# An adaLN transformer block on one core: packed head rows, 11-matmul output projections, and where two of four blocks are projected

## The chip, the cores and the metric

The kernel runs on one core of a Trainium2 chip. The metric is the device time of one execution in microseconds. The engines are named as in the profile: PE (TensorE, matmuls), PEld (the weight loads of TensorE), DVE (VectorE), ACT (ScalarE), POOL (GpSimd) and SP (SyncE, which here only issues DMAs).

## The reference, cut to what matters

One sequence of 2048 tokens with 448 features passes through attention with 16 heads of 28 and then through an MLP of width 1792. Both are modulated by six rows computed from a condition `c`:

```python
sa, ca, ga, sb, cb, gb = (silu(c) @ w_mod).reshape(1, 6, 1, 448) rows
h = layernorm(x) * (1 + ca) + sa
x = x + ga * (softmax_attention(h, wqkv, heads=16) @ wo)     # heads side by side: 448 columns
h = layernorm(x) * (1 + cb) + sb
x = x + gb * (gelu(layernorm(h) @ w1 + b1) @ w2 + b2)
```

The change touches the product of the attention's output with `wo` and the addition to `x`.

## The kernel before, in words

**Precision.** Large products run in the fp32r format. An operand is split into `hi` (the value rounded to fp32r) and `lo` (the rest), and a product is summed as hi·hi + hi·lo + lo·hi. So each piece of 128 contracted rows costs three matmuls.

**Phase 1** (the first 166 us of the profile) computes the modulation, the layernorm, the queries, keys and values, and a first part of the row maxima of the scores. Queries and keys go through DRAM, in tiles that hold four heads, each head in 32 rows of which 28 are data.

**Attention** is a loop of 16 units of 16 steps (`for u in range(NU)`, L1271). Unit `u` is head group `g = u // 4` (four heads) and query block `qt = u % 4` (512 tokens); its 16 steps `kt` go over tiles of 128 keys. Below, a step's number is `16 * u + kt`, 0 to 255. A step issues 12 score matmuls (L1305) into two PSUM pairs, two exponentials on ACT (L1318), between them some matmuls whose only use is a later row maximum (L476, reduced on DVE at L481), and then the four products with the values (L1263, `av`) of the step before. Everything else hangs on steps through `at(step, fn)` and a dictionary `sched`: after the `av` of a step, the functions planned for it are emitted. All instructions of an engine run in the order of emission; waits come from data and buffers.

From step 121 on (`RING`) a third PSUM pair is in use for the scores, except in the steps for which `is_wo` holds (L1239): there the third pair is given back, so that its two banks can take other matmuls. When no maxima are left (`three`), the third pair is used throughout. Which maxima go into which step is set by `extra` and `emit_single`, three of them in a step of this phase.

**End of a unit** (`unit_end_tasks`, L995). The unit's output, 4 heads by 32 rows by 512 queries, of which row 28 of each head holds the softmax's denominators, is normalised in four tasks: `t_den` and `t_rec` send the denominators through DRAM and broadcast their reciprocals, `t_split` multiplies (POOL, L1019), `t_split2` makes `hi` (DVE if the unit's output is stored, ACT if not, L1029) and `lo` (POOL, L1030). For groups 0 to 2 the pair is stored to DRAM (`doh`, L1034: two DMAs of 128 rows, gap rows included), except unit (2, 3), whose output stays on chip. Stored units run their tasks 1, 4, 10 and 11 steps into the next unit, the others 1, 2, 6 and 7.

**Output projection before** (`t_wo`, L1036). When the last group of a query block is normalised, the three stored groups of that block have been loaded again (`load_o`, six DMAs of 256 KB, L992), and four chains, one for each 128 tokens, multiply them with `wo_p`, which is `wo` with `ga` folded in, in the same layout of four heads in 128 rows with gaps. A chain has 4 groups of 3 terms, 12 matmuls of 128 rows by 448 columns; ACT copies it out of PSUM (L1052) and POOL adds it to the residual `acc` (L1053). Blocks 0, 1 and 2 are projected at `kt` 8 to 11 of units 13, 14 and 15, one chain in a step. Block 3 has two parts: the groups 0 to 2 (9 matmuls a chain) at `kt` 8 to 11 of unit 12, and group 3 (3 matmuls a chain) after the attention.

**MLP** (L1398). `seq` goes over 4 blocks of 14 slices, and iteration `n` emits `mlp1` of slice `n` (11 matmuls of 512 columns, L396 and L1347, then GELU), the functions that `tail` holds for `n`, one or two items of weight preparation (`w_prep`: load, split into hi and lo), the next block's layernorm stages, and `mlp2` of slice `n - 2` (12 matmuls of 448 columns, L1389 to L1391). The first `mlp1` is emitted before the last `av`. `tail` holds the eight tasks of the last unit: before, at `n` = 0, 0, 4, 5 for the normalising and 9, 10, 11, 12 for the four chains of 3. The PSUM banks for `mlp1`, for chains and for transposes are a ring of three.

**Weight preparation** starts in unit 15 (`w_prep`, L1220): ten of its items are done in steps 245 to 255, each with a load two items ahead into a ring of three `raw` buffers, then two or three operations on DVE (L1150, L1151, L1169 to L1172). Items go into the slots that attention leaves (`a0` to `e1`), so a slot that is taken for something else must be free again by its item. SP issues every one of these DMAs in order, and stops at the first that has to wait.

Of the kernel before, what the change touches and what calls it, by code (L numbers as in the profile page):

```python
# [44 lines left out]
def tile_adaln_block(ctx: ExitStack, tc: tile.TileContext, x, wqkv, wo, w1, b1, w2, b2, c, w_mod, out):  # L45
# [72 lines left out]
    def f(t):  # L118
        return t.bitcast(F32)
# [834 lines left out]
                self.n += 1  # L954
            self.load(self.n + 2)

    def wo_item(g):
        def ld(r):
            pool.memset(r[:, :D], 0.0)
            for j in range(4):  # L960
                hd = 4 * g + j
                sp.dma_start(r[32 * j : 32 * j + DH, :D], wo[DH * hd : DH * hd + DH, :])

        def go(r):
            full = sbt("full", [128, 512], bufs=3)
            pool.tensor_tensor(out=full[:, :D], in0=r[:, :D], in1=rows["ga"], op=ALU.mult)

            def rest():
                dve.tensor_copy(wo_p[0][:, g, :], full[:, :D])
                pool.tensor_tensor(out=wo_p[1][:, g, :], in0=full[:, :D], in1=f(wo_p[0])[:, g, :], op=ALU.subtract)  # L970

            at(6 + 2 * g, rest)

        return ld, go

    doh = [
        [dr.tile([128, S], F32R, tag=f"o{part}{g}", name=f"o{part}{g}", bufs=1) for g in range(NG - 1)]  # L980
        for part in range(2)
    ]
    o_in = {}

    def last_g(qt):
        return NG - 2 if qt == NB - 1 else NG - 1

    def load_o(qt):
        for g, tag in zip(range(last_g(qt)), ("a2h", "a3h", "b1h")):
            t = slot(tag, [128, 2, 512])  # L990
            for part in range(2):
                sp.dma_start(f(t)[:, part, :], f(doh[part][g])[:, qt * 512 : (qt + 1) * 512])  # L992
            o_in[(qt, g)] = t

    def unit_end_tasks(u, o_sb):  # L995
        g, qt = divmod(u, NB)
        st = {}
        staged = g < last_g(qt)
        parts = [g] if g > last_g(qt) else list(range(g + 1))

        def t_den():
            q_ = pool if u == NU - 1 else sp
# [18 lines left out]
        def t_split2():  # L1021
            on = st["on"]
            if u < NU - 1:
                hi = sbt("hi", [128, 512], F32R, bufs=3)
                lo = sbt("lo", [128, 512], F32R, bufs=3)
            else:
                hi = sb.tile([128, 512], F32R, tag=YTAGS[7], name="o_hi", bufs=1)
                lo = sbt("osb", [128, 512], F32R, bufs=2)
            (dve.tensor_copy if staged else act.copy)(hi, on)  # L1029
            pool.tensor_tensor(out=lo, in0=on, in1=f(hi), op=ALU.subtract)  # L1030
            st["hi"], st["lo"] = hi, lo
            if staged:
                for part in range(2):
                    sp.dma_start(f(doh[part][g])[:, qt * 512 : (qt + 1) * 512], f((hi, lo)[part]))  # L1034

        def t_wo(t):  # L1036
            def go():
                if t == 3 and mx_ring[0] == "m1" and len(mx_ring) > 1:
                    mx_ring.append(mx_ring.pop(0))
                p = ps_mx()  # L1040
                ts = slice(t * 128, (t + 1) * 128)
                terms = []
                for g_ in parts:
                    if g_ == g:
                        hi, lo = st["hi"][:, ts], st["lo"][:, ts]
                    else:
                        hi, lo = o_in[(qt, g_)][:, 0, ts], o_in[(qt, g_)][:, 1, ts]
                    w_hi, w_lo = wo_p[0][:, g_, :], wo_p[1][:, g_, :]
                    terms += [(hi, w_hi), (hi, w_lo), (lo, w_hi)]
                mm_acc(p[:, :D], terms)  # L1050
                y = sbt("full", [128, 512], bufs=3)[:, :D]
                act.copy(y[:, :D], p[:, :D])  # L1052
                pool.tensor_tensor(out=acc[qt][:, t, :], in0=acc[qt][:, t, :], in1=y[:, :D], op=ALU.add)  # L1053

            return go

# [123 lines left out]
    def at(step, fn):  # L1180
        sched.setdefault(step, []).append(fn)

    wo_prep = Prep([wo_item(g) for g in range(NG)])
    at(0, lambda: wo_prep.load(2))
    for g in range(NG):
        at(4 + 2 * g, wo_prep.step)

    def b2_load():
        rows["b2"] = raw_t()
# [13 lines left out]
    at(12, b2_load)  # L1203
    at(28, b2_mul)
    last0 = NKT * (NU - 1)
    lnst = [ln2_stages(b) for b in range(NB)]
# [134 lines left out]
    def mlp1(b, i):  # L1341
# [114 lines left out]
```

## Time and profile before

| what | us |
|---|---|
| median of 3 runs (1108.62 to 1109.58) | 1109.07 |
| the profiled execution, its own time | 1109.11 |
| its span, from the first to the last instruction | 1107.1 |
| steps 0 to 255 of attention | 166.7 to 812.9 |
| MLP after it | 812.9 to 1107.1 |

The granted clock of TensorE was 1.0 throughout. A busy share of PE is not PE at its peak, since matmuls are pipelined: what a stage costs is read from the time between the same instruction of one step and of the next. Times in rows are microseconds from the span's start; a group's row has its count, the busy time, the mean duration in ns, and the idle time before it with what ended it.

### The profile page before, as it was taken

Reading aid. Unit: us, or ns where it says so; the run is one execution under the profiler, and the core shown is the slowest. Engines: PE = TensorE matmul, PEld = TensorE weight load, DVE = VectorE, ACT = ScalarE, POOL = GpSimd, SP = SyncE. Lnnn points to the kernel's source line nnn. Section 1 sums busy time; section 2 is a strip of 40 time slices with the busy share of each in tenths; the row PEclk is TensorE's granted clock in tenths of the full one; section 3 lists DMA queues with packets and bytes.
Section 4 is the critical chain, followed back from the end, with each engine's and each line's share of the span. In section 5 each row is a group of like instructions: output and inputs, shape, how many; then the busy total and the mean of one; then the engine's idle time right before and its main releaser. Section 6 shows DMA issues by size and latency. Waiting matters only on the chain.

```text
span 1107.1 us, 20699 instructions
## 1 busy us (share of the span) xinstructions
PE 1097.3 (99%) x8319; PEld 666.5 (60%) x8319; DVE 799.5 (72%) x1375; ACT 703.8 (64%) x897; POOL 212.4 (19%) x214
## 2 busy tenths in 40 slices
PE   8999999999999999999999999999999999999998
PEld 6756675444444444444444454545568888888887
DVE  6968788999899989988888868584557744534322
ACT  4565667888888888888888878687764411111210
POOL 1543333110000000000000011216215414023000
PEclk9999999999999999999999999999999999999999
DMA  9563263121221201231211412022222100000000
GB/s 309 206 188 107 90 199 112 56 68 30 79 87 50 78 30 49 69 96 49 75 44 47 137 30 87 1 87 72 78 82 67 31 34 1 7 28 1 34 1 34
DMA packets 49341, 81.19 MB, mean 73 GB/s; under 512 B 12311, under 2 KB 18702, under 8 KB 49234
## 3 DMA queue, kind: packets, MB, share of 16 engines
q1 hardware_dynamic: 48762, 79.14, 22.9%
q8 instruction: 65, 1.06, 0.4%
q10 hardware_dynamic: 148, 0.46, 0.1%
q0 software_dynamic: 336, 0.28, 0.1%
q14 instruction: 30, 0.25, 0.1%
HBM read 55.04 MB, written 26.48 MB: 74 GB/s over the span
## 4 chain that ended last, share of the span: by engine, by line
PE 97%; DVE 1%; DMA 1%; ACT 1%; issue 0%; SPq 0%; ACTq 0%; DVEq 0%
PE o L1263 23%; PE s L1305 23%; PE m L396 17%; PE pa L396 9%; PE m L476 8%; PE s L1390 3%; PE s L1391 3%; PE s L1389 3%; PE s L476 2%; PE t L1390 1%; PE t L1391 1%; PE t L1389 1%; DMA slot_c<-in_w_mod_dram 1%; PE o L277 1%; DVE mxp L481 1%; PE ma L476 0%
## 5 line engine op out<-in xcount | busy, mean ns | idle before, releaser
L481 DVE TENSOR_REDUCE mxp<-m 128x1 f32<-128x512 f32 x563 | 364.6, 685 | 75.0 <-PE m L476 56.2
L1305 PE MATMUL s<-slot_b,slot_a 28*128 28x512 f32 (+1 forms) x3072 | 356.7, 423 | 0.3 <-ACT slot_c0h L1318 0.3
L1305 PEld LDWEIGHTS s<-slot_b,slot_a 28*128 28x128 f32 (+1 forms) x3072 | 210.7, 184 | 171.9 <-ACT slot_c L1318 93.9
L476 PE MATMUL m<-kh,qh 28*128 28x512 f32 x615 | 228.2, 468 | 0.5 <-DVE mxp L481 0.3
L1318 ACT ACTIVATE slot_c<-s 128x1024 f32<-128x1024 f32 x170 | 174.7, 1028 | 52.4 <-PE s L1305 51.7
L1263 PE MATMUL o<-slot_c,v 128*32 128x512 f32 x680 | 178.9, 605 | 0.0
L1351 ACT ACTIVATE full<-m,b_col 128x512 f32<-128x512 f32 x56 | 38.5, 688 | 193.7 <-PE m L396 172.5
L1263 PE MATMUL o<-slot_c1h,v 128*32 128x512 f32 x512 | 134.7, 605 | 0.0
L1263 PE MATMUL o<-slot_c0h,v 128*32 128x512 f32 x512 | 134.7, 605 | 0.0
L1318 ACT ACTIVATE slot_c0h<-s 128x1024 f32<-128x1024 f32 x128 | 131.7, 1029 | 2.5 <-PE m L396 2.5
L1318 ACT ACTIVATE slot_c1h<-s 128x1024 f32<-128x1024 f32 x128 | 130.8, 1022 | 0.0
L686 DVE TENSOR_REDUCE mxp<-s 128x2 f32<-128x1024 f32 x103 | 126.2, 1225 | 4.9 <-PE s L1305 0.3
L1354 DVE CAST hi<-full 128x512 fp32r<-128x512 f32 x42 | 18.6, 443 | 121.2 <-ACT full L1351 121.2
L1318 ACT ACTIVATE slot_d<-s 128x1024 f32<-128x1024 f32 x86 | 88.4, 1028 | 25.6 <-PE s L1305 25.5
L476 PEld LDWEIGHTS m<-kh,qh 28*128 28x128 f32 x615 | 91.5, 182 | 15.8 <-DVE mxp L481 13.4
L1263 PE MATMUL o<-slot_d,v 128*32 128x512 f32 x344 | 90.5, 605 | 0.4 <-ACT osb L1227 0.4
L1019 POOL TENSOR_TENSOR osb<-osb,osb 128x512 f32<-128x512 f32 x16 | 20.5, 1283 | 363.3 <-DMA osb<-drec 197.2
L396 PE MATMUL m<-y,slot_a 128*128 128x512 f32 x160 | 60.7, 395 | 0.0
L1355 DVE TENSOR_TENSOR lo<-full,hi 128x512 fp32r<-128x512 f32 x56 | 41.7, 745 | 20.5 <-ACT hi L1354 16.6
L481 DVE TENSOR_REDUCE mxp<-ma 128x1 f32<-128x512 f32 x61 | 39.5, 681 | 13.2 <-PE m L476 8.1
L650 DVE CUSTOM_DVE_ANT_0 slot_d0i<-m,slot_d0i 128x512 f32<-128x512 f32 x54 | 37.3, 691 | 15.2 <-PE m L476 11.4
L1263 PEld LDWEIGHTS o<-slot_c,v 128*32 128x32 f32 x680 | 24.5, 108 | 39.3 <-issue 36.8
(344 smaller groups left out, 1855.3 us busy)
## 6 DMA issues: line engine op xcount, KB each, us to landing
slot_b<-d SPq DMA_DIRECT2D x32, 256.0 KB
slot_a<-d SPq DMA_DIRECT2D x32, 256.0 KB
d<-lo SPq DMA_DIRECT2D x28, 256.0 KB
d<-hi SPq DMA_DIRECT2D x16, 256.0 KB
osb<-drec SPq DMA_DIRECT2D x15, 256.0 KB
out_dram<-xn SPq DMA_DIRECT2D x16, 224.0 KB
raw<-in_B_w_dram SPq DMA_DIRECT2D x14, 224.0 KB
qh<-d SPq DMA_DIRECT2D x12, 256.0 KB
```

The costliest lines, as they stand in the source:

```text
L396: pe.matmul(p, a, b, start=(i == 0), stop=(i == len(terms) - 1))
L476: pe.matmul(m, qh_sb[(g, qt)][js, i * 128 : (i + 1) * 128], k[js, :], start=True, stop=True)
L481: dve.tensor_reduce(out=mxp[(g, qt)][:, i, j, cch : cch + 1], in_=m, op=ALU.max, axis=AX.X)
L686: dve.tensor_reduce(out=mxp[(g, qt)][:, i, j : j + 2, cch], in_=t, op=ALU.max, axis=AX.X)
L1263: pe.matmul(o[32 * j : 32 * j + 32, :], v_sb[kt // 4][:, kt % 4, 4 * g + j, :], p[j // 2][:, j % 2, :], start=(kt == 0), stop=(kt == NKT - 1),
L1305: pe.matmul(s2[:, jj, :], ks[rows_, kp, kc], qs[rows_, qp, :], start=(term == 0), stop=(term == 2))
L1318: act.activation(pt[hf], s2, AF.Exp, scale=SCALE)
L1351: act.activation(gf, p, AF.Gelu_apprx_tanh, bias=b1_col[:, i : i + 1])
L1355: dve.tensor_tensor(out=glo, in0=gf, in1=f(ghi), op=ALU.subtract)
L1389: pe.matmul(pp, ghi[:, ts], w_hi, start=(m == 0), stop=False)
L1390: pe.matmul(pp, ghi[:, ts], w_lo, start=False, stop=False)
L1391: pe.matmul(pp, glo[:, ts], w_hi, start=False, stop=(m == NFT - 1))
```

## The change

Stored heads are packed: `dpk` in DRAM has 28 rows for each of the 12 stored heads, 336 in all, for `hi` and for `lo`. The 336 rows are two full tiles of 128 and a rest of 80. The rest's three terms are mixed into two operands: one has 80 rows of `hi` and 48 of `lo`, the other 32 rows of `lo` and 80 of `hi`, each with the fitting rows of `wo`. So a chain has 6 + 2 matmuls for the stored heads and 3 for the last group, which keeps its gaps: 11. `wo` is prepared in five items with the same layout.

Storing a unit takes four DMAs of 28 rows for each of `hi` and `lo` in place of one of 128. A block is loaded with one DMA for the full tiles of `hi`, one for those of `lo`, and four for the mixed operands.

Blocks 0 and 1 stay in units 13 and 14. Unit (2, 3) is now stored like the others, and no chain runs in unit 12. Unit (3, 2), the one with number 14, is stored too (`down`), no chain runs in unit 15, and block 2 is projected with four chains of 11 at `n` = 1 to 4 of the MLP; its mixed operands and `down` are loaded, just ahead of the first `mlp1`, into slots that the exponentials used (`c1`, `c0h`). Block 3 is projected with four chains of 11 at `n` = 6, 7, 8 and 8. For blocks 2 and 3 DVE adds the chain in PSUM to `acc` itself. `is_wo` holds in units 13 and 14 alone. `b2_load` moves from step 12 to 15.

```diff
+    NP = (NG - 1) * 4 * DH
+    MIX_HI = ((256, NP), (256, 304))
+    MIX_LO = ((304, NP), (256, NP))
...
+    dpk = [dr.tile([NP, S], F32R, tag=f"o{part}", name=f"o{part}", bufs=1) for part in range(2)]
+    down = [dr.tile([128, 512], F32R, tag=f"w{part}", name=f"w{part}", bufs=1) for part in range(2)]
...
+    def load_o(qt, n, tag):
+        t = slot(tag, [128, 2, 512])
+        o_in[(qt, n)] = t
+        cs = slice(qt * 512, (qt + 1) * 512)
+        if n < 2:
+            sp.dma_start(f(t), f(dpk[n])[0:256, cs].rearrange("(k p) n -> p k n", p=128))
+        elif n == 2:
+            for k, pieces in enumerate((zip((0, 1), MIX_HI), zip((1, 0), MIX_LO))):
+                p0 = 0
+                for part, (r0, r1) in pieces:
+                    sp.dma_start(f(t)[p0 : p0 + r1 - r0, k, :], f(dpk[part])[r0:r1, cs])
+                    p0 += r1 - r0
+        else:
             for part in range(2):
+                sp.dma_start(f(t)[:, part, :], f(down[part]))
+
+    def wo_terms(qt, own):
+        hi, lo, mix = (o_in[(qt, n)] for n in range(3))
+        w_hi, w_lo = wo_p
+        terms = []
+        for k in range(2):
+            terms += [(hi[:, k], w_hi[:, k, :]), (hi[:, k], w_lo[:, k, :]), (lo[:, k], w_hi[:, k, :])]
+        terms += [(mix[:, 0], w_hi[:, 2, :]), (mix[0:112, 1], w_lo[0:112, 2, :])]
+        o_hi, o_lo = own
+        return terms + [(o_hi, w_hi[:, 3, :]), (o_hi, w_lo[:, 3, :]), (o_lo, w_hi[:, 3, :])]
+
+    def project(qt, t, own):
+        p = ps_mx()
+        ts = slice(t * 128, (t + 1) * 128)
+        mm_acc(p[:, :D], [(x[:, ts], w) for x, w in wo_terms(qt, own)])
+        if qt >= NB - 2:
+            dve.tensor_tensor(out=acc[qt][:, t, :], in0=p[:, :D], in1=acc[qt][:, t, :], op=ALU.add)
+            return
+        y = sbt("full", [128, 512], bufs=3)[:, :D]
+        act.copy(y, p[:, :D])
+        pool.tensor_tensor(out=acc[qt][:, t, :], in0=acc[qt][:, t, :], in1=y, op=ALU.add)
...
-        staged = g < last_g(qt)
-        parts = [g] if g > last_g(qt) else list(range(g + 1))
+        staged = g < NG - 1 or qt == NB - 2
...
             if staged:
                 for part in range(2):
-                    sp.dma_start(f(doh[part][g])[:, qt * 512 : (qt + 1) * 512], f((hi, lo)[part]))
+                    src = f((hi, lo)[part])
+                    if g == NG - 1:
+                        sp.dma_start(f(down[part]), src)
+                        continue
+                    for j in range(4):
+                        r0 = DH * (4 * g + j)
+                        sp.dma_start(
+                            f(dpk[part])[r0 : r0 + DH, qt * 512 : (qt + 1) * 512], src[32 * j : 32 * j + DH, :]
+                        )
...
-    for u in range(NU - NB - 1, NU - 1):
-        at(NKT * (u + 1) - 3, lambda qt=u % NB: load_o(qt))
+    for qt in range(NB - 2):
+        for n, tag in enumerate(("a2h", "a3h", "b1h")):
+            at(NKT * (NU - NB + qt + 1) - 3, lambda qt=qt, n=n, tag=tag: load_o(qt, n, tag))
+    for n, tag in enumerate(("a3h", "b1h")):
+        at(NKT * (NU - 1), lambda n=n, tag=tag: load_o(NB - 2, n, tag))
...
     def is_wo(s_):
-        return s_ // NKT >= NU - NB and 8 <= s_ % NKT < 12
+        return NU - NB < s_ // NKT < NU - 1 and 8 <= s_ % NKT < 12
...
+    load_o(NB - 2, 2, "c1")
+    load_o(NB - 2, 3, "c0h")
     mlp1(0, 0)
     av(*pend)
     end_unit(pend[0], pend[3])
     tail = {}
     assert len(sched) == 8
-    for n, k in zip((0, 0, 4, 5, 9, 10, 11, 12), sorted(sched)):
+    for t in range(4):
+        tail[1 + t] = [lambda t=t: project(NB - 2, t, [o_in[(NB - 2, 3)][:, part] for part in range(2)])]
+    tail[1].append(lambda: load_o(NB - 1, 1, "c1h"))
+    tail[4] += [lambda: load_o(NB - 1, 0, "c1"), lambda: load_o(NB - 1, 2, "b1h")]
+    for n, k in zip((0, 0, 4, 5, 6, 7, 8, 8), sorted(sched)):
         tail.setdefault(n, []).extend(sched[k])
```

More of the change, by code (lines that the diff above doesn't have):

```diff
@@ L964, in go @@
         def go(r):
             full = sbt("full", [128, 512], bufs=3)
-            pool.tensor_tensor(out=full[:, :D], in0=r[:, :D], in1=rows["ga"], op=ALU.mult)
+            ps = slice(0, 112 if n == 3 else 128)
+            pool.tensor_tensor(out=full[ps, :D], in0=r[ps, :D], in1=rows["ga"][ps], op=ALU.mult)
             def rest():
-                dve.tensor_copy(wo_p[0][:, g, :], full[:, :D])
-                pool.tensor_tensor(out=wo_p[1][:, g, :], in0=full[:, :D], in1=f(wo_p[0])[:, g, :], op=ALU.subtract)
@@ L972, in go @@
-            at(6 + 2 * g, rest)
+                if n == 3:
+                    hi = sbt("hi", [128, 512], F32R, bufs=3)
+                    dve.tensor_copy(hi[ps, :D], full[ps, :D])
+                    pool.tensor_tensor(out=wo_p[1][ps, 2, :], in0=full[ps, :D], in1=f(hi)[ps, :D], op=ALU.subtract)
+                    pool.tensor_copy(wo_p[1][0:32, 2, :], f(hi)[0:32, :D])
+                    return
+                k = min(n, 3)
+                dve.tensor_copy(wo_p[0][:, k, :], full[:, :D])
@@ L974, in wo_item @@
+                if n != 2:
+                    pool.tensor_tensor(out=wo_p[1][:, k, :], in0=full[:, :D], in1=f(wo_p[0])[:, k, :], op=ALU.subtract)
+            at(6 + 2 * n, rest)
         return ld, go
[L979 to L982, printed above, removed]
+    dpk = [dr.tile([NP, S], F32R, tag=f"o{part}", name=f"o{part}", bufs=1) for part in range(2)]
+    down = [dr.tile([128, 512], F32R, tag=f"w{part}", name=f"w{part}", bufs=1) for part in range(2)]
@@ L1039, in go @@
                     mx_ring.append(mx_ring.pop(0))
[L1040 to L1053, printed above, removed]
+                project(qt, t, (st["hi"], st["lo"]))
             return go
@@ L1181, in at @@
         sched.setdefault(step, []).append(fn)
-    wo_prep = Prep([wo_item(g) for g in range(NG)])
+    wo_prep = Prep([wo_item(n) for n in range(5)])
     at(0, lambda: wo_prep.load(2))
-    for g in range(NG):
-        at(4 + 2 * g, wo_prep.step)
+    for n in range(5):
+        at(4 + 2 * n, wo_prep.step)
     def b2_load():
@@ L1202, in tile_adaln_block @@
         at(6 + g, lambda g=g: put_ones(g))
-    at(12, b2_load)
+    at(15, b2_load)
     at(28, b2_mul)
```

22 lines of the change are left out of this document (10 added, 12 removed).

## The prediction

> **What bounds the kernel now.** I read the page first: the busy shares and the chain that ended last.
>
> ```profile
> span 1107.1 us, 20699 instructions
> PE 1097.3 (99%) x8319; PEld 666.5 (60%) x8319; DVE 799.5 (72%) x1375; ACT 703.8 (64%) x897; POOL 212.4 (19%) x214
> PE 97%; DVE 1%; DMA 1%; ACT 1%; issue 0%; SPq 0%; ACTq 0%; DVEq 0%
> ```
>
> TensorE is on the chain for 97% of the span. That doesn't yet say that a matmul less is a matmul's time less, since a busy TensorE also covers waits inside a pipelined stage. So I took the timeline of TensorE, found where each step's first score matmul starts, and cut the span there. Two successive steps of unit 12, each with one chain of 9:
>
> ```profile
> 650.52 0.49 PE L1305 MATMUL s<-slot_b,slot_a 29*128 29x512 f32 x2
> ...
> 654.83 0.50 PE L1305 MATMUL s<-slot_b,slot_a 29*128 29x512 f32 x2
> ```
>
> The windows view over such cuts then gives the price of a step. The rows are, in order: steps 136 to 199 (no chain, three maxima each), steps 200 to 203 (unit 12, chains of 9), steps 216 to 219 and 232 to 235 (units 13 and 14, chains of 12), steps 248 to 251 (unit 15, chains of 12, no maxima left) and steps 252 to 255 (no chain).
>
> ```profile
> core 0: us, PE busy (x) PEld busy (x) DVE busy (x) ACT busy (x) POOL busy (x), PEclk, DMA share, GB/s
> 506.68:650.52 143.84, 143.84 (x1477) 62.20 (x1474) 125.09 (x147) 125.68 (x133) 11.72 (x12) 1.00 0.23 70
> 650.52:667.30 16.78, 16.78 (x132) 10.37 (x128) 7.97 (x13) 10.41 (x13) 4.72 (x4) 1.00 0.02 4
> 694.15:713.41 19.26, 19.26 (x145) 12.68 (x141) 7.98 (x13) 10.56 (x13) 4.73 (x4) 1.00 0.00 1
> 740.90:760.34 19.44, 19.44 (x142) 12.61 (x138) 9.87 (x23) 10.55 (x13) 8.07 (x8) 1.00 0.05 8
> 786.76:804.94 18.18, 18.18 (x129) 11.43 (x129) 10.64 (x17) 10.71 (x14) 4.74 (x4) 1.00 0.29 84
> 804.94:812.90 7.96, 7.96 (x82) 3.09 (x81) 3.52 (x6) 7.37 (x9) 1.36 (x1) 1.00 0.34 101
> ```
>
> And the score matmuls alone in the first and the last of these, at 12 in a step: 768 are 64 steps, 48 are four (one record straddles the cut).
>
> ```profile
> 506.68:650.52 143.84, 84.53 (x769) 51.32 (x770) 1.00 0.23 70
> ...
> 804.94:812.90 7.96, 4.21 (x48) 2.42 (x48) 1.00 0.34 101
> ```
>
> So a plain step costs 143.84 / 64 = 2.25 us, and four steps with chains of 9 cost 16.78 instead of 8.99. A chain isn't hidden beside the exponentials: the step gets longer by the whole chain. The clock was 1.00 in all of these rows, so no term below depends on it.
>
> **The change part by part.** *One matmul.* The chains alone in units 12 and 13:
>
> ```profile
> 650.52:667.30 16.78, 8.30 (x36) 6.44 (x36) 1.00 0.02 4
> 694.15:713.41 19.26, 10.78 (x48) 8.69 (x48) 1.00 0.00 1
> ```
>
> 12 matmuls more are 2.48 us busy, and 19.26 - 16.78 = 2.48 us of window: 0.207 us each in attention.
>
> *Unit 12 loses its four chains of 9.* Its steps become plain ones that keep the third PSUM pair and still take three maxima: 16.78 - 4 x 2.25 = 7.8 us saved. The total of maxima stays, so I expect them to end at the same step as now.
>
> *Units 13 and 14* keep their chains, shorter by one matmul: 8 x 0.207 = 1.65 us saved. Copy, addition and due steps stay.
>
> *Unit 15 loses four chains of 12.* The nearest plain steps are the next four, 7.96 us. But ScalarE now matters, because its share there is already 7.37 of 7.96. What it did in the chain steps beside the exponentials:
>
> ```profile
> L1052 ACT COPY full<-m 128x448 f32<-128x448 f32 x3 | 1.6, 533 | 4.9 <-PE m L396 4.9
> ...
> L1029 ACT CAST hi<-osb 128x512 fp32r<-128x512 f32 x1 | 0.6, 640 | 0.0
> L1118 ACT CAST y<-m 128x512 fp32r<-128x512 f32 x1 | 0.6, 595 | 0.0
> ```
>
> The copies of the chains go, the cast of `hi` goes to VectorE and three steps later, the cast of `y` (0.6 us) stays and has lost its cover. So four steps cost between 7.96 and 8.56; I take 8.3, and save 18.18 - 8.3 = 9.9 us (9.6 to 10.2).
>
> *The MLP gains* 8 x 11 - 4 x 3 = 76 matmuls. The present chain of 3 stands between `mlp1` and `mlp2`, and so will the new ones:
>
> ```profile
> 860.00 0.40 PE L396 MATMUL m<-y,slot_a 128*128 128x512 f32 x1
> ...
> 862.57 0.57 PE L396 MATMUL m<-slot_e,o_hi 128*128 128x448 f32 x2
> 862.98 0.37 PE L396 MATMUL m<-slot_e,osb 128*128 128x448 f32 x1
> 863.19 0.37 PE L1389 MATMUL s<-slot_d,hi 128*128 128x448 f32 x1
> ...
> 865.64 0.39 PE L396 MATMUL m<-y,slot_a 128*128 128x512 f32 x1
> ```
>
> The 11 of `mlp1` take 2.57 us, the 3 of the chain 0.62 (0.207 each), the 12 of `mlp2` after them 2.45 (0.204 each). I take 0.205: 76 x 0.205 = 15.6 us added. VectorE adds the chains from PSUM, as it adds the MLP's result now:
>
> ```profile
> L1395 DVE TENSOR_TENSOR xn<-s,acc 128x448 f32<-128x448 f32 x12 | 6.6, 616 | 0.1
> ```
>
> That is 0.62 us a chain, and the iteration gets longer by a chain of 2.3 us at the same time, so I cost it at nothing. Without that cover the PSUM ring of three would stop TensorE by at most the 0.6 us of one addition, eight times.
>
> *The entry of the first chain.* Block 2's chains need operands that can be loaded only when attention's last buffers come free. The weight loads of TensorE around the end of attention:
>
> ```profile
> 812.90 0.19 PEld L396 LDWEIGHTS m<-y,slot_b 128*128 128x128 f32 x1 [0.84 <-issue]
> ...
> 815.65 0.11 PEld L1263 LDWEIGHTS o<-slot_c1h,v 128*32 128x32 f32 x2 [0.37 <-ACT full L1350]
> ...
> 816.64 0.19 PEld L396 LDWEIGHTS m<-y,slot_b 128*128 128x128 f32 x1 [0.84 <-issue]
> ```
>
> On this clock `c1` and `c0h` are free at 812.9, when the product of step 254 has ended and the first `mlp1` starts. The second `mlp1` starts at 816.64 and ends 2.57 us later, at 819.2; the first chain follows. Its six first matmuls use loads from step 240, so it needs the mixed operands at 820.4 and `down` at 820.8. Six DMAs of much that size on SP, and the one 256 KB DMA whose landing the page gives:
>
> ```profile
> 758.60 0.80 SPq L992 DMA_DIRECT2D slot_a2h<-o  x2
> 759.43 0.90 SPq L992 DMA_DIRECT2D slot_a3h<-o  x2
> 760.44 0.84 SPq L992 DMA_DIRECT2D slot_b1h<-o  x2
> ...
> osb<-drec POOLq DMA_DIRECT2D x1, 256.0 KB, 5.9
> ```
>
> Six issues take 2.7 us, so the last leaves at 815.6. With 5.9 us it lands at 821.5, 0.7 late; with less it is in time. I take 0.3 us of wait, between 0 and 0.7. The Trainium skill (DMA: Bandwidth & Descriptors, section "Anatomy of one DMA — SWDGE (gpsimd) path") fits 2.0 us plus the bytes over 436 GB/s, an estimate of 2.6 us for 256 KB; by it the wait would be 0 and the sum 0.3 us lower. The row of 5.9 is a broadcast from DRAM and speaks for more, so I keep my value between the two.
>
> *Stores and loads of packed heads.* Each stored unit issues eight DMAs of 28 rows instead of two. The 28-row DMAs that load `wo` now, and what follows a store on SP:
>
> ```profile
> 179.21 1.68 SPq L962 DMA_DIRECT2D raw<-in_A_wo_dram  x4
> ...
> 402.04 0.33 SPq L1034 DMA_DIRECT2D o<-lo  x1
> ...
> 413.61 0.58 SPq L1004 DMA_DIRECT2D den<-osb  x1
> ```
>
> At 0.42 us each, eight are 3.4 us, 2.5 more than now by the same 0.42; SP has 11 us before it issues again. Cost: nothing. The five items of `wo` take 10 DMAs instead of 16 and one more cast on VectorE (about 0.4 us, once, in a step pair with room): nothing.
>
> *Block 3* is projected three iterations earlier. Today's `lo` of the last unit:
>
> ```profile
> 839.39 1.76 POOL L1030 TENSOR_TENSOR osb<-osb,o_hi 128x512 fp32r<-128x512 f32 x1
> ...
> 841.79 0.37 PE L1389 MATMUL s<-slot_v,hi 128*128 128x448 f32 x1
> ```
>
> It is done at 841.15, within iteration 6, whose `mlp1` ends at 841.79, where `mlp2` begins. The new chain starts there and needs `lo` only in its 11th matmul, 2 us later: no wait, with 2.7 us of room. Its loaded operands are asked for when block 2's last chain ends, in iteration 4, two `mlp1` and two `mlp2` (10 us) ahead.
>
> **The sum.** Saved 7.8 + 1.65 + 9.9 = 19.35; added 15.6 + 0.3 = 15.9; net -3.45 us. About 3.3 of it are the 16 matmuls that no longer exist; moving the rest is nearly neutral. The profiled execution took 1109.11 (2.0 around its span), the median is 1109.07, so one base serves both: 1109.1 - 3.5 = 1105.6 us.
>
> **Rivals.** *The first chain waits longer.* SP issues in order, and ahead of those six DMAs stand the stores of `down` and the loads for weight preparation, each of which waits for VectorE. For it: VectorE has 10.64 + 3.52 = 14.2 us of work from 786.76 to 812.90, and the stretch shrinks from 26.1 to about 16.3 us. Against: part of today's delay is a wait that disappears,
>
> ```profile
> 797.75 0.62 DVE L1169 TENSOR_TENSOR full<-raw,row_gb 128x448 f32<-128x448 f32 x1 [3.65 <-POOL acc L1053]
> ```
>
> since no chain uses the `full` ring in unit 15 any more. A slip of 2 to 4 us makes a wait of 1 to 3.5 us: 1106.5 to 1108.9.
>
> *The same slip, and the kernel is slower.* If VectorE and SP come 7 us or more late at that point (waits of the raw loads on top of its work), TensorE stands before the mixed operands for over 5.7 us, which takes back 3.5 and another 2.2: 1111.5 or more. It decides from a landing at about 826 on the old clock.
>
> *Unit 15's steps stay longer.* Steps 248 to 251 now run next to weight preparation without the slack of the chains. If they take 2.5 us in place of 2.07, the saving is 1.7 us less: 1107.3.
>
> *The chains in attention ran in time that was free.* Then their removal saves nothing but the units' 1.65, and the MLP pays 15.6: 1123. The weight loads are busy for only 62.20 of 143.84 us in plain steps. The Trainium skill (Perfetto Trace Analysis, section "Identifying the Most-Contended Engine") says that matmul busy time is no good measure of TensorE and asks for the share of weight loads; by it attention would look half idle. The rows of 16.78 against 8.99 and 18.18 against 7.96 speak against it as strongly as rows can.
>
> *The change brings more:* steps at 7.96, no wait, 0.204 a matmul: 1104.9 or a little lower.
>
> **How the numbers follow.** Forecast (1104.9 to 1106.5) 0.66; more 0.06; first chain waits 0.13; unit 15 longer 0.08; slip to slower 0.05; free time 0.02. A difference of 0.2%, 2.2 us, is about what a measurement of this kernel can tell from none. Below 1106.9 lie the forecast, the better case, half of the waiting case and a little of unit 15's: 0.80. Within 0.2%: 0.13. Slower: 0.07. The range 1104.2 to 1107.8 takes in the ends of the unknown terms and the nearer part of both waiting cases, and leaves out some 0.14.
>
> **What would show each step right or wrong.** In the new profile the starts of score matmuls should be 2.25 us apart at `kt` 8 to 11 of unit 12 and 2.0 to 2.1 in unit 15; the chain steps of units 13 and 14 should lose 0.2 us each; a chain of 11 in the MLP should take 2.25 us from its first matmul to the next instruction's. The weight load before the seventh matmul of the first chain shows the entry: idle time there, released by a DMA, is the waiting rival. If the gain is missing without idle time there, look at steps 244 to 255 and at the MLP's iterations 1 to 8 for a longer pitch.

## The result and the profile after

| | before | after |
|---|---|---|
| median of 6 runs each | 1109.07 (1108.61 to 1109.58) | 1103.66 (1102.99 to 1104.77) |
| the profiled execution, its own time | 1109.11 | 1104.08 |
| its span | 1107.1 | 1102.0 |

The ratio is 0.9953, with a 95% interval of 0.9942 to 0.9963: faster by 5.4 us, where 3.5 was forecast, and below the low end of the range (1104.2). Run again beside three experiments, the changed kernel took 1103.51 (1103.40 to 1104.91, 5 runs) against 1108.72 of the kernel before.

The page after, its span, busy shares and chain that ended last:

```profile
span 1102.0 us, 20732 instructions
PE 1092.8 (99%) x8303; PEld 664.3 (60%) x8303; DVE 799.0 (73%) x1382; ACT 697.2 (63%) x883; POOL 196.7 (18%) x201
PE 97%; DVE 1%; DMA 1%; ACT 1%; issue 0%; SPq 0%; ACTq 0%; DVEq 0%
```

There are 16 matmuls fewer, and TensorE is on the chain for the same 97%. The bound has not moved to another engine; the time must be looked for inside its stages. The windows view of the kernel after, cut at the same steps as before: plain steps 136 to 199, unit 12's steps 200 to 203, unit 13's chain steps 216 to 219, step 220, unit 14's chain steps 232 to 235, and unit 15's steps 248 to 251.

```profile
506.54:650.30 143.76, 143.76 (x1477) 62.07 (x1474) 125.12 (x147) 125.72 (x133) 10.44 (x11) 1.00 0.21 61
650.30:659.30 9.00, 9.00 (x96) 3.92 (x92) 7.77 (x9) 7.73 (x9) 1.29 (x1) 1.00 0.01 2
686.21:704.67 18.46, 18.46 (x140) 11.99 (x136) 8.21 (x15) 10.55 (x13) 4.76 (x5) 1.00 0.02 2
704.67:706.85 2.18, 2.18 (x24) 0.86 (x23) 1.53 (x2) 1.71 (x3) 1.15 (x1) 1.00 0.80 235
731.52:750.40 18.88, 18.88 (x137) 12.04 (x134) 10.16 (x23) 10.56 (x13) 8.20 (x8) 1.00 0.01 1
776.81:784.79 7.98, 7.98 (x81) 3.10 (x81) 6.22 (x12) 7.76 (x10) 1.28 (x1) 1.00 0.46 135
```

Plain steps cost what they did (143.76 against 143.84), so the stages can be compared one by one. Unit 12 and unit 15 now run at the pitch of steps without chains. Step 220 was not among the rows of before; here it is:

```profile
713.41:716.21 2.80, 2.41 (x27) 0.88 (x26) 2.24 (x4) 2.33 (x3) 1.18 (x2) 1.00 0.00 0
```

It took 2.80 us and takes 2.18. The two ends of the program, cut at the first score matmul of step 0 and of step 192, and from that of step 255 to the end of the last matmul; first before, then after:

```profile
166.69:632.46 465.77, 465.29 (x4536) 213.72 (x4535) 416.18 (x679) 400.06 (x451) 44.08 (x51) 1.00 0.22 67
810.85:1103.18 292.33, 291.78 (x1380) 249.95 (x1376) 136.07 (x246) 69.97 (x114) 61.68 (x51) 1.00 0.08 24
```

```profile
166.84:632.26 465.42, 465.04 (x4536) 213.38 (x4535) 416.85 (x680) 399.91 (x451) 44.61 (x50) 1.00 0.23 64
790.72:1098.12 307.40, 307.04 (x1456) 264.18 (x1452) 136.72 (x258) 68.66 (x110) 54.29 (x47) 1.00 0.11 34
```

The tail has 76 matmuls more and takes 15.07 us more. Its entry, in the weight loads of TensorE and the DMA issues of SP after:

```profile
798.93 0.42 PEld L396 LDWEIGHTS m<-slot_e,slot_a3h 128*128 128x128 f32 x2
...
800.17 0.39 PEld L396 LDWEIGHTS m<-slot_e,slot_c 128*128 128x128 f32 x2
800.57 0.61 PEld L396 LDWEIGHTS m<-slot_e,slot_c0h 128*128 128x128 f32 x3
801.19 0.19 PEld L396 LDWEIGHTS m<-y,slot_b 128*128 128x128 f32 x1
```

```profile
793.79 1.93 SPq L1011 DMA_DIRECT2D slot_c<-o  x4
795.83 0.83 SPq L1015 DMA_DIRECT2D slot_c0h<-w  x2
```

No weight load of the chain has idle time before it: the mixed operands (`slot_c`) and the staged `down` (`slot_c0h`) were there. The chain takes 801.19 - 798.93 = 2.26 us.

Set against the sum of the prediction, in us (negative is saved; the last column is after minus before, from the rows above and those shown of before):

| term | predicted | measured |
|---|---|---|
| unit 12, steps 200 to 203 | -7.8 | 9.00 - 16.78 = -7.78 |
| units 13 and 14, chain steps | -1.65 | (18.46 - 19.26) + (18.88 - 19.44) = -1.36 |
| step 220 | 0 | 2.18 - 2.80 = -0.62 |
| unit 15, steps 248 to 251 | -9.9 | 7.98 - 18.18 = -10.20 |
| MLP and its entry | +15.9 | 307.40 - 292.33 = +15.07 |
| steps 0 to 191 | 0 | 465.42 - 465.77 = -0.35 |
| start of step 0 | 0 | 166.84 - 166.69 = +0.15 |
| the other steps | 0 | the rest, about 0 |
| **sum** | **-3.45** | **-5.06**, the end of the last matmul (1098.12 - 1103.18) |

### The profile page after: what moved, and what is told of

Same layout as the page of the kernel before. It is cut to its first block, busy times and chain, and to the rows that moved or that the text cites. A ratio compares the mean times of both kernels' runs of the same rounds, so it can differ in the third digit from the quotient of the medians.

```text
span 1102.0 us, 20732 instructions
## 1 busy us (share of the span) xinstructions
PE 1092.8 (99%) x8303; PEld 664.3 (60%) x8303; DVE 799.0 (73%) x1382; ACT 697.2 (63%) x883; POOL 196.7 (18%) x201
## 4 chain that ended last, share of the span: by engine, by line
PE 97%; DVE 1%; DMA 1%; ACT 1%; issue 0%; SPq 0%; ACTq 0%; DVEq 0%
PE s L1345 23%; PE o L1303 23%; PE m L396 17%; PE pa L396 9%; PE m L476 8%; PE s L1436 3%; PE s L1437 3%; PE s L1435 3%; PE s L476 2%; PE t L1436 1%; PE t L1437 1%; PE t L1435 1%; DMA slot_c<-in_w_mod_dram 1%; PE o L277 1%; DVE mxp L481 0%; PE ma L476 0%
## 5 line engine op out<-in xcount | busy, mean ns | idle before, releaser
L481 DVE TENSOR_REDUCE mxp<-m 128x1 f32<-128x512 f32 x555 | 359.9, 686 | 65.6 <-PE m L476 48.1
L686 DVE TENSOR_REDUCE mxp<-s 128x2 f32<-128x1024 f32 x107 | 131.2, 1226 | 5.0
L481 DVE TENSOR_REDUCE mxp<-ma 128x1 f32<-128x512 f32 x61 | 39.5, 682 | 13.2 <-PE m L476 7.9
L650 DVE CUSTOM_DVE_ANT_0 slot_d0i<-m,slot_d0i 128x512 f32<-128x512 f32 x54 | 37.3, 691 | 14.4 <-PE m L476 10.5
```

What stands on the lines that cost most here:

```text
L481: dve.tensor_reduce(out=mxp[(g, qt)][:, i, j, cch : cch + 1], in_=m, op=ALU.max, axis=AX.X)
L686: dve.tensor_reduce(out=mxp[(g, qt)][:, i, j : j + 2, cch], in_=t, op=ALU.max, axis=AX.X)
```

## The experiments

Theory: the time is TensorE's stage by stage, so packing is worth a matmul's 0.2 us sixteen times, moving the chains is nearly neutral, and what the sum missed is small effects next to the chains: the order of the row maxima and a wait at the entry that did not come. Rivals: the moving itself brings more than the sum has, or the entry was much further from waiting than the sum assumes.

### Block 2 back in unit 15

```diff
-        return NU - NB < s_ // NKT < NU - 1 and 8 <= s_ % NKT < 12
+        return NU - NB < s_ // NKT and 8 <= s_ % NKT < 12
...
-    for t in range(4):
-        tail[1 + t] = [lambda t=t: project(NB - 2, t, [o_in[(NB - 2, 3)][:, part] for part in range(2)])]
```

Its loads and its eviction by ACT and POOL go back as well; only block 3 stays in the MLP.

> Packed heads stay, block 2 goes back into unit 15 (chains of 11, added by ScalarE and GpSimd), block 3 stays in the MLP. Theory (a moved chain is worth the difference between its price in an attention step and its price in the MLP, 2.27 us): steps 248 to 251 go back from 7.98 to about 17.3 us, the MLP loses four chains, 9.1 us; so 0.3 us slower than the changed kernel, about 1104.0. Rival (the 2 us beyond the forecast come from moving block 2): about 1105.5 or more.

Measured: 1103.86 us (1103.58 to 1105.17, 5 runs), ratio 0.9951 (0.9939 to 0.9963). Its steps 248 to 251, in the windows view:

```profile
776.46:793.84 17.38, 17.38 (x126) 10.70 (x125) 10.39 (x17) 10.70 (x14) 4.95 (x4) 1.00 0.31 85
...
799.75:1098.16 298.41, 298.05 (x1412) 255.86 (x1408) 133.41 (x250) 68.67 (x110) 56.37 (x47) 1.00 0.10 29
```

17.38 - 7.98 = 9.40 us for four chains of 11, 2.35 each. In the MLP, from step 255 to the last matmul (the second row), the same four chains cost 307.40 - 298.41 = 8.99. So moving block 2 is worth some 0.4 us, too little to tell in the medians, and the theory holds: most of the gain does not come from here. But for the account of the prediction it counts. By its terms this move would have cost 0.3 us: four steps at 8.3 in place of 18.18 less four matmuls (17.35), 44 matmuls at 0.205 in the MLP (9.02), and 0.3 of wait. So some 0.7 us of the miss lie in block 2's move, in unit 15's steps and at the entry.

### Moved, but not packed

```diff
-    dpk = [dr.tile([NP, S], F32R, tag=f"o{part}", name=f"o{part}", bufs=1) for part in range(2)]
+    doh = [
+        [dr.tile([128, S], F32R, tag=f"o{part}{g}", name=f"o{part}{g}", bufs=1) for g in range(NG - 1)]
+        for part in range(2)
+    ]
...
-        terms += [(mix[:, 0], w_hi[:, 2, :]), (mix[0:112, 1], w_lo[0:112, 2, :])]
```

The layout with gap rows, two stores a unit and chains of 12; the chains stand where the change puts them.

> Both blocks are moved as in the changed kernel, but heads are stored with gap rows and chains have 12 matmuls. Theory (packing is worth one matmul of 0.206 us in each of 16 chains and nothing else): 3.3 us slower than the changed kernel, about 1107.0, with a chain of 12 in the MLP at 2.47 us and the chain steps of unit 13 back at 4.78. Rival (moving carries most of the gain, 3 us or more): 1105.5 or less. Second rival (the packed layout's short stores and loads cost time, so that packing is worth less): 1104 to 1106, with steps 0 to 191 shorter than in the changed kernel.

Measured: 1107.18 us (1106.93 to 1108.08, 11 runs), ratio 0.9982 (0.9973 to 0.9991). Its MLP with the end of attention, from step 255 to the last matmul, and its unit 13:

```profile
792.66:1101.86 309.20, 308.84 (x1464) 265.61 (x1460) 136.70 (x258) 68.67 (x110) 54.24 (x47) 1.00 0.11 34
686.56:705.84 19.28, 19.28 (x144) 12.76 (x140) 8.23 (x15) 10.58 (x13) 4.76 (x5) 1.00 0.04 8
```

309.20 against 307.40 is 1.8 us for eight matmuls more, 19.28 against 18.46 is 0.8 for four. Against the kernel before on the same chip, 1109.26 - 1107.18 = 2.1 us belong to moving (the interval of the ratio allows 1.0 to 3.0), and what is left of the 5.4, some 3.3, to packing. The prediction had 0.15 and 3.3: **the miss lies in the moving**. By the experiment before, some 0.7 us of it are block 2's; the others must be block 3's, whose first part left unit 12.

### Unit 12 without its third pair

```diff
-        return NU - NB < s_ // NKT < NU - 1 and 8 <= s_ % NKT < 12
+        return NU - NB <= s_ // NKT < NU - 1 and 8 <= s_ % NKT < 12
```

No chain comes back; the steps 200 to 203 only give the third PSUM pair back and take their maxima as before the change.

> The changed kernel, but steps 200 to 203 are planned like steps with a chain (third PSUM pair given back), without a chain in them. Theory (the 0.6 us by which step 220 got shorter come from the other order of the maxima after unit 12 ran with three pairs): step 220 is 2.8 us again, the four steps cost up to 0.5 us more, 1104.3 to 1104.8. Rival (step 220 got shorter because the chain ahead of it did): step 220 stays at 2.2 us, 1103.7 to 1104.2.

Measured: 1104.51 us (1104.50 to 1105.06, 5 runs), ratio 0.9957 (0.9944 to 0.9969). The reductions of row maxima in DVE's line L481, by the windows view over step 220 and unit 14's chain steps (length, busy time and count); before, after, and this kernel:

```profile
713.41:716.21 2.80, 1.37 (x2) 1.00 0.00 0
740.90:760.34 19.44, 5.03 (x8) 1.00 0.05 8
```

```profile
704.67:706.85 2.18, 0.69 (x1) 1.00 0.80 235
731.52:750.40 18.88, 5.63 (x9) 1.00 0.01 1
```

```profile
704.94:707.74 2.80, 1.37 (x2) 1.00 0.02 6
732.43:751.07 18.64, 5.03 (x8) 1.00 0.01 1
```

With unit 12's steps in the old form, step 220 has its second reduction of this kind and its 2.80 us again, and unit 14 loses the ninth. So the steps of unit 12 set where the last maxima of the units after them fall. Before, step 220 holds four maxima where a plain step holds three (two of them in one reduction, L686), and TensorE waits there:

```profile
714.77 0.49 PE L476 MATMUL s<-kh,qh 28*128 28x512 f32 x2 [0.39 <-DVE mxp L481]
```

The fourth moved into step 234, beside a chain of unit 14: it saves 0.62 us in step 220 and costs 18.88 - 18.64 = 0.24 in unit 14. The kernel that is not packed has the new form of unit 12 too, and its step 220 takes 2.18 us, so packing has no part in this. The third pair itself saves time in unit 12:

```profile
649.86:659.64 9.78, 9.78 (x97) 4.32 (x94) 8.13 (x14) 8.08 (x9) 1.29 (x1) 1.00 0.01 2
```

9.78 against 9.00 with no chain in either: 0.78 of the 7.78 saved in unit 12 is the pair, 7.0 the chains.

### Block 2's chains one iteration earlier

```diff
-        tail[1 + t] = [lambda t=t: project(NB - 2, t, [o_in[(NB - 2, 3)][:, part] for part in range(2)])]
+        tail[t] = [lambda t=t: project(NB - 2, t, [o_in[(NB - 2, 3)][:, part] for part in range(2)])]
```

TensorE reaches the first chain 2.4 us sooner, so its loads are sure to be late, and one can see by how much.

> The changed kernel with block 2's four chains one iteration earlier (n = 0 to 3), so that TensorE reaches the first chain at about 796.5 on the changed kernel's clock and asks for the mixed operands at 797.7 and for the last group's at 798.1, 2.4 us earlier than now; the last of their six DMAs is issued at 796.2. Theory (loads land about 3 us after issue): TensorE waits about 1 us in that chain, 1104.7. Rival A (they land 5.9 us after issue, as the one row of the page says): a wait of 4 us, 1107.7. Rival B (they land before they are asked for even then): no wait, 1103.7.

Measured: 1107.04 us (1104.99 to 1108.50, 11 runs), ratio 0.9977 (0.9968 to 0.9986). The matmuls of TensorE around the first chain, and the issues on SP:

```profile
796.51 0.67 PE L396 MATMUL m<-slot_e,slot_a3h 128*128 128x448 f32 x2
...
799.29 0.47 PE L396 MATMUL m<-slot_e,slot_c 112*128 112x448 f32 x1 [0.82 <-DMA slot_c<-o]
800.76 1.12 PE L396 MATMUL m<-slot_e,slot_c0h 128*128 128x448 f32 x3 [1.00 <-DMA slot_c0h<-w]
...
802.61 0.63 PE L396 MATMUL m<-y,slot_a 128*128 128x512 f32 x1
803.03 0.63 PE L396 MATMUL m<-y,slot_b 128*128 128x512 f32 x1
```

```profile
794.55 1.93 SPq L1011 DMA_DIRECT2D slot_c<-o  x4
796.59 0.83 SPq L1015 DMA_DIRECT2D slot_c0h<-w  x2
```

The first DMA of `down` was issued at 796.59 and its operand used at 800.76: 4.2 us. On these 4.2 it lands in the changed kernel at 795.83 + 4.2 = 800.0, an estimate, and the chain asks for it at 800.57. The second DMA (`lo`, needed in the last matmul of the chain) has less room, as the repeat of the changed kernel shows below. But the wait is only part of the loss. The windows of the chain, and of the product that follows it, in two halves:

```profile
796.51:801.53 5.02, 3.15 (x15) 1.83 (x12) 0.69 (x1) 1.52 (x3) 0.91 (x1) 1.00 0.81 281
801.53:803.46 1.93, 1.93 (x6) 1.54 (x7) 0.78 (x2) 0.00 (x0) 0.00 (x0) 0.67 0.35 124
803.46:805.60 2.14, 2.14 (x7) 1.65 (x6) 1.35 (x4) 0.00 (x0) 0.59 (x1) 0.50 0.19 24
```

The chain took 5.02 us, 2.76 more than 2.26. The product of 11 matmuls behind it took 1.93 + 2.14 = 4.07, and there the granted clock is 0.67 and 0.50: its matmuls start 0.42 us apart, where 0.23 is usual. That is another 1.5 us, in which nothing waits. So the number is near rival A's, but not for its reason: the landing lies between the theory's 3 us and rival A's 5.9, and the clock is in none of the three. The profile is of the slowest of the 11 executions (1108.50).

### The same entry without the wait

```diff
+        if own is None:
+            mix, own = hi, (hi[:, 0], hi[:, 1])
...
-project(NB - 2, t, [o_in[(NB - 2, 3)][:, part] for part in range(2)])
+project(NB - 2, t, [o_in[(NB - 2, 3)][:, part] for part in range(2)] if t else None)
```

> Block 2's four chains stand behind iterations 0 to 3 of the MLP, as in the earlier entry, but the first of them takes the loaded high tile of block 2 again where it should take the mixed operands and the staged heads of unit 14, so it waits for no late load; its 128 rows of the output are therefore not the reference's. The count of matmuls is the same. In the earlier entry the first chain took 5.02 us where it takes 2.27, and the product after it 4.07 at a granted clock of 0.67 and 0.50. Theory: the product was slow because the clock fell after TensorE had stood still for 1.9 us of 799.0 to 801.5; without the standstill there is no fall, and the time is the changed kernel's, 1103.7 within 0.5, the first chain 2.3 us, the product after it 2.5 at a clock of 1.00. Rival: the place of the chain behind the product of iteration 0 is dear in itself (the weights of the product, the additions on VectorE, or the transfers that run beside it); then the product after it stays at 3.5 us or more, and the time is 1105 or above.

Measured: 1103.56 us (1102.96 to 1103.97, 5 runs), ratio 0.9953 (0.9939 to 0.9966). The windows of the last `av` with the first chain, and of the product behind it:

```profile
794.99:798.13 3.14, 3.14 (x20) 2.15 (x20) 0.69 (x1) 2.31 (x4) 0.84 (x1) 1.00 0.77 204
798.13:800.66 2.53, 2.53 (x13) 2.06 (x11) 0.62 (x1) 0.00 (x0) 0.07 (x1) 1.00 0.91 334
```

The `av` takes 1.00 us of the first window and the chain 2.14. Without the standstill the clock stays at 1.00 and the product takes 2.53 us. The place is not dear; the wait is, and the clock after it. The theory holds. Against the 2.14 us of this chain, at the same place, the chain of the earlier entry lost 5.02 - 2.14 = 2.9 us.

### The changed kernel again

No edit; it is the pair of the kernels with the earlier entry without the wait, the other eviction and the cut stores.

> The changed kernel unaltered, as the pair to the three kernels beside it. All theories: 1103.7 us, within 0.5 (six executions so far lay between 1103.0 and 1104.8), span 1101 to 1102.5.

Measured: 1103.51 us (1103.40 to 1104.91, 5 runs), ratio 0.9956 (0.9944 to 0.9968), with a span of 1101.4 in its profile. Its step 0 starts at 166.08, that of the changed kernel's first profile at 166.84; the steps 192 to 255 agree within 0.03 us a stage. The weight loads of the first chain and behind it:

```profile
798.19 0.42 PEld L396 LDWEIGHTS m<-slot_e,slot_a3h 128*128 128x128 f32 x2
...
800.43 0.19 PEld L396 LDWEIGHTS m<-slot_e,slot_c0h 128*128 128x128 f32 x1 [0.19 <-DMA slot_c0h<-w]
800.54 0.19 PEld L396 LDWEIGHTS m<-y,slot_b 128*128 128x128 f32 x1
```

Here the last weight load of the chain does wait for `down`, and the chain takes 800.54 - 798.19 = 2.35 us in place of 2.26. So the changed kernel stands at the edge of this wait: one profile has none of it, the other 0.1 us.

### Blocks 2 and 3 evicted by ScalarE and GpSimd

```diff
-        if qt >= NB - 2:
+        if qt >= NB:
```

> Chains of blocks 2 and 3 leave PSUM as those of blocks 0 and 1 do, by a copy on ScalarE and an addition on GpSimd, in place of one addition on VectorE. Theory (prediction: the eviction has cover of a whole chain): no change, 1103.7 within 0.5, chains still 2.27 us. Rival: VectorE's addition is what keeps the MLP's bounds short. ScalarE also applies the exponential-like function of each iteration, and GpSimd took 1.3 us for an addition of 128x512 in attention; the normalisations of blocks 2 and 3 would start later, and TensorE would wait for them: 1104.5 to 1107, with idle time of TensorE at the products that follow the two blocks' normalisation.

Measured: 1103.99 us (1103.95 to 1104.63, 5 runs), ratio 0.9959 (0.9947 to 0.9972), beside 1103.51 of the changed kernel; their ranges lie over each other. From step 255 to the last matmul the profile of this kernel has 307.57 us, the changed kernel's second profile 307.53. The eviction's engine makes no difference to TensorE, as the prediction costed it.

### Stores cut in two

```diff
-                        sp.dma_start(
-                            f(dpk[part])[r0 : r0 + DH, qt * 512 : (qt + 1) * 512], src[32 * j : 32 * j + DH, :]
-                        )
+                        for c in range(2):
+                            cs = slice(256 * c, 256 * c + 256)
...
```

> Each of the eight stores of a packed unit is cut into two of 28 rows by 256 columns (28 KB each), so that a unit issues 16 DMAs. At 0.42 us an issue that is 6.7 us on SP per unit instead of 3.4, with some 11 us before SP issues the next thing. Theory (prediction: the stores cost nothing): 1103.7 within 0.5. Rival: the small DMAs crowd the queue, by the row lengths of 1 KB in place of 2 KB and the later issue of the loads behind them; then loads of the next unit land late and TensorE waits in attention: 1104.5 or more. The Trainium skill (DMA: Bandwidth & Descriptors, section Rules for kernel authors) calls DMAs under 64 KB mostly overhead; by it the 16 would cost the queue about twice the time of the eight.

Measured: 1106.97 us (1104.52 to 1109.60, 11 runs), ratio 0.9981 (0.9972 to 0.9991). The expectation of no change falls, and the rival's 1104.5 or more holds. Two more kernels split the loss by place, one with 16 stores in unit 11 only, one with 16 in all units but that:

```diff
+                        w = 256 if u == 11 else 512     # the other kernel: u != 11
+                        for c in range(0, 512, w):
```

> Only the stores of unit 11 (block 3, third group of heads), which SP issues in unit 12, are cut into 16 of 28 KB; all other units keep eight. With 16 everywhere the kernel took 1106.97 us (1104.5 to 1109.6), and in its profile SP issued the 16 from 659.93 to 668.05, the three loads of block 0 until 671.24, and the DMA of the sums (den) at 671.35; its landing ended an idle 0.98 us of VectorE before the reciprocal at 676.08, and step 212 took 2.92 us in place of 2.15. Before unit 12 the reciprocal comes 7.6 to 9.5 us after that DMA's issue, in units 13 and 14 3.6 us. Theory: the place just ahead of the reciprocal that is due early, in unit 13, makes the whole loss: about 1106.5, between 1105.5 and 1107.5, with idle time of VectorE before the reciprocal in step 212. Rival: each unit's 16 stores cost a little; then this is near the changed kernel, 1103.6 to 1104.2.

> The complement: all stored units but unit 11 are cut into 16 DMAs. Theory (the loss is made by unit 11's stores alone): 1103.6 within 0.6, no idle time of VectorE before a reciprocal other than the last. Rival (each unit costs a little, or the small rows do): 1105.5 to 1107.

Measured: unit 11 only, 1105.12 us (1103.95 to 1105.49, 5 runs), ratio 0.9962 (0.9947 to 0.9976); all but unit 11, 1106.21 us (1105.05 to 1109.69, 11 runs), ratio 0.9977 (0.9968 to 0.9986). One place does not make the whole, so the theory of both expectations falls. The second number lies where its rival put it, but the same small cost in each unit isn't the account either, since unit 11 alone makes some 1.6 (beside 1103.51). DVE in step 212 of the kernel with unit 11's 16 stores, and SP ahead of it:

```profile
673.79 1.23 DVE L686 TENSOR_REDUCE mxp<-s 128x2 f32<-128x1024 f32 x1
676.89 0.25 DVE L1052 RECIPROCAL den<-den 128x16 f32<-128x16 f32 x1 [1.88 <-DMA den<-osb]
```

```profile
659.50 3.32 SPq L1084 DMA_DIRECT2D o<-hi  x8
662.93 4.59 SPq L1084 DMA_DIRECT2D o<-lo  x8
667.56 0.39 SPq L1006 DMA_DIRECT2D slot_a2h<-o  x1
...
671.23 0.59 SPq L1046 DMA_DIRECT2D den<-osb  x1
```

The stores and, behind them, block 0's loads are issued right up to the DMA of the denominators. That DMA leaves in time, but lands later, DVE stands 1.88 us before the reciprocal, and the maxima queued behind it, which TensorE needs, are late: step 212 takes 3.80 us where it takes 2.15 in the changed kernel. In the kernel with 16 stores in the other units the place is step 32, where the keys of the next unit are loaded right behind the stores:

```profile
244.13 3.32 SPq L1084 DMA_DIRECT2D o<-lo  x8
247.55 0.82 SPq L508 DMA_DIRECT2D kh<-d  x2
```

The same load in the changed kernel:

```profile
243.00 1.65 SPq L1082 DMA_DIRECT2D o<-lo  x4
244.75 0.82 SPq L508 DMA_DIRECT2D kh<-d  x2
```

The profile of the kernel with 16 stores in the other units has TensorE waiting 0.2 us for that load, and step 32 takes 3.41 us in place of 2.77. That is 0.6 of its loss of 2.7. Its first chain in the MLP waits 0.4 us for its loads, and its step 0 starts at 167.33, 1.25 later than in the repeat of the changed kernel, ahead of every store that was cut. With 16 everywhere, steps 32 and 212 together are 1.3 us longer, but that profile is of the fastest execution, 1104.52. So of the 3.5 us in its median the larger part isn't seen in a profile. The executions above 1107.4 of both kernels had a mean granted clock of 0.996 to 0.998, so they held stretches at a lower clock. Where, no profile shows; that part stays open. The Trainium skill (DMA: Bandwidth & Descriptors, section "Rules for kernel authors") calls transfers under 64 KB mostly overhead. The issues agree: a store of 28 KB takes SP 3.32 / 8 = 0.42 us, as one of 56 KB does (1.65 / 4 = 0.41).

## Why the prediction was too careful

The direction and the mechanism held: TensorE bounds every stage, a chain costs its whole length wherever it stands, and no other engine took the bound. Point by point:

- **Unit 12:** -7.8 forecast, -7.78 measured.
- **The step that failed** is the term of the row maxima, put at nothing with the sentence beside it: "The total of maxima stays, so I expect them to end at the same step as now." Both are so: the traces count 838 maxima under L481 and L686 before and after, and the last stand in step 234 in both. But it doesn't follow that nothing changes between. The experiment on unit 12 shows that the form of its steps moves a maximum out of step 220: -0.62 there, +0.24 in unit 14, net -0.4. Step 220 had no term in the sum, and its 2.80 us before were not looked at. This is the only mechanism that the sum left out and an experiment isolates, but it is a quarter of the miss of 1.6 us between -3.45 and -5.06. The others are terms that were mis-sized: unit 15 and the entry by 0.3 each, the rest of the MLP by 0.5, and steps 0 to 191, put at nothing, by 0.35 (the start of step 0 gave 0.15 back).
- **Units 13 and 14:** -1.65 forecast. Unit 13 gave 0.80 and unit 14 0.56; in the kernel whose maxima stay, unit 14 gives 19.44 - 18.64 = 0.80. So one matmul is 0.2 us in both, as costed, and the missing 0.24 is the maximum that moved in.
- **Unit 15:** 8.3 us forecast for four steps, 7.98 measured, the low end. The cast of `y` lost its cover, as said, but cost nothing: ACT is busy for 7.76 of 7.98 us and still does not hold TensorE.
- **Entry:** 0.3 us forecast, none measured in the first profile, 0.1 in the repeat. The sum took the landing as 5.9 at most; the earlier entry shows 4.2. The rival in which the first chain waits for 1 us or more did not come true, and of its slip only 1.0 us: SP began the six DMAs at 793.79, when the first product had started at 792.75. The shorter landing just made up for that, which was luck: with 5.9 and this slip the wait would have been about 1.7, an estimate.
- **MLP:** 15.6 forecast for 76 matmuls, against 15.07 for the whole tail. A chain at 2.26 us is 0.205 a matmul, as forecast. Summed from start to start of matmuls in the traces, the chains take 17.87 us after (88 matmuls, 0.203 each) and 2.46 before, 15.41 more. Outside them TensorE waits 0.36 us for normalised rows at the start of the second block in place of 0.54, and the products of `mlp2` are some 0.2 us shorter together, which differs from profile to profile. With block 2 back in unit 15 the tail falls short in the same way, 298.41 - 292.33 = 6.08 for 32 matmuls more (6.56 at 0.205), so this 0.5 is not block 2's.
- **Steps 0 to 191:** -0.35, without a term. The repeat and the other packed kernels whose early stores are not cut (465.36 to 465.55 us in their profiles) agree on it and the kernel that is not packed has 465.69, so it goes with the packing. Most of it sits in steps 50 and 51: 5.02 to 5.05 us packed, 5.27 not packed, 5.29 before. Its cause stays open.
- **Stores:** costed at nothing, and nothing was measured, but the reason given was read at one place. "SP has 11 us before it issues again" is true of the unit quoted; in unit 1 the load of the next keys stands 0.1 us behind the stores, and in unit 12 the loads of block 0 do. The cut stores show that eight issues more a unit would have cost 3.5 us in the median.

The range was too narrow below. The entry and unit 15 were set between their ends and came out at the cheap end, the maxima, the rest of the tail and steps 0 to 191 had no term, and all five errors went the same way. The case in which all goes well was put at 1104.9, with the chance 0.06; its conditions (steps at 7.96, no wait) came true, and the time went lower still by the terms that were missing. Beside that, the start of step 0 lies at 165.93 to 167.33 in the profiles of this study, a spread of 1.4 us that one profiled execution does not show. In the rival that ends slower, 3.5 taken back and another 2.2 make 1111.3, not 1111.5; nothing hangs on it. No experiment points to a version that beats the changed kernel.

## What to carry to other kernels

Cut the trace of a TensorE-bound kernel at the same instruction of each stage and write one term per stage, those that the change doesn't touch included: here the surprise sat in a step that nothing was removed from. Before a queue's extra issues are costed at nothing, look at every place where they fall, not at one: what counts is the tightest, and what stands right behind. When work is moved, ask what order the neighbours' other work takes, since the same maxima in other steps cost or save as much as a small term. And if all unknown terms are set to their middle or dear end, the range must still reach to where all of them go well.

## What the runs showed of the hardware

**A short standstill can cost twice.** In the profile of the earlier entry TensorE stood for 0.82 and 1.00 us inside 2.5 us, waiting for loads. Its matmuls then started 0.42 us apart in place of 0.23, from about 802.2 to 805.6, some 3.4 us at a granted clock of 0.50. Without the wait the clock stayed at 1.00. Of the 11 executions with the wait, the five from 1107.86 to 1108.50 had a mean granted clock of 0.998 and the six from 1104.99 to 1107.04 one of 0.999 or 1.0, so the fall seems not to come each time; only one of them was profiled. The Trainium skill (TensorE: Matmul & The Clock Gate, section "HAM oscillation — how this bites in real kernels") has as its rule that no idle gap of TensorE should be longer than about 3.4 us; here two gaps, of 1.0 us at most, were enough. In the profile after, two waits for loads of 0.85 and 0.60 us, ended at 8.9 and 10.5 us, were followed by no fall: the granted clock is 1.00 from there to the last matmul. Where the limit lies, no run here shows.

**Landing of 256 KB on SP's queue, with other loads beside it:** 4.2 us from issue to use, for the first DMA of `down` in the earlier entry. The Trainium skill (DMA: Bandwidth & Descriptors, section "Anatomy of one DMA — SWDGE (gpsimd) path") has a fit for another queue that gives 2.6, an estimate.

**Stages repeat, the start does not.** Unit 12's steps 200 to 203 take 8.97 to 9.00 us in the ten profiles that have them in the new form, and unit 15's steps 248 to 251 take 7.96 to 7.98 in the ten without chains there. The start of step 0 varies by 1.4 us over the profiles of this study.
